# Attention's steps ahead of gl, weight sums in three chunks, first loads of sums moved, in an attention and FFN kernel

## The chip, the cores and the metric

The kernel runs on one core of a Trainium2 chip. The metric is the time of one execution on the device, in microseconds. TensorE multiplies matrices, VectorE and ScalarE work elementwise, GpSimd does a few reductions and exchanges, and SyncE (SP) issues the DMA transfers. Each engine works through a list of its own; a wait at the head of a list holds what stands behind it.

## The reference

Inputs are q, k and v of shape (8, 8, 576, 64): batch, heads, sequence, head dimension; and two weights, `w_in` (512, 2048) and `w_out` (2048, 512). All is float32.

```python
def _attn_ref(q, k, v):
    q_s = softmax of q over the head dimension
    k_s = softmax of k over the sequence
    kv = np.einsum('bhsd,bhse->bhde', k_s, v)
    return np.einsum('bhsd,bhde->bhse', q_s, kv)

x = attn_out.transpose(0, 2, 1, 3).reshape(8 * 576, 512)
h = np.maximum(x @ w_in, 0.0)
return h * h @ w_out
```

(The two softmax lines stand for the subtraction of the maximum, the exponential and the division by the sum plus 1e-9.) The attention is linear: it needs one 64x64 block `kv` for each head, and then one product with q. The two products of the FFN are nearly all of the arithmetic.

## The kernel before

**The numbers.** A float32 product is done as three matmuls of pieces: each operand is split into a rounded high part and the rest (`xh` and `xl`, `gh` and `gl`, and the weights alike), and high by high, high by low and low by high are added up.

**The tiles.** The 4608 rows of x are cut into nine tiles of 512: eight of the first 512 positions of a batch, and one of the eight tails of 64. Tiles t = 0 to 4 (`WT = 5`) run the FFN plainly. For each of 16 slabs f of 128 columns of the hidden layer: `first` multiplies x by a slab of w_in (12 matmuls into a bank `h`; there are two such banks); `split_g` makes `r` (the relu, ScalarE), its square (ScalarE), the high part `gh` (a cast on ScalarE), and `gl = r - gh` (VectorE); `second` multiplies by a slab of w_out and adds into four banks `acc`. `second` runs two slabs behind (`LA = 2`), so a `gl` has two slabs of time until it is read. `gh` has two buffers.

**The joint blocks.** Tiles 5, 6 and 7, 8 form two joint blocks of 1024 rows. They use a scheme of seven products for a 2x2 product of blocks (Strassen and Winograd), with sums of blocks of x and of weights as operands. `first_products(k)` runs pairs n = 0 to 7 of slabs, seven products each; `second_products(k)` the product by w_out. The sums of weights are made once, in tiles 1 to 3, for three keys a tile (`KEYS`), and stored in DRAM as `w_sums` and `wo_sums`: `full_sums` (two additions of 128x512), `add_sums` (four of 128x256), `split_sums` (two casts on ScalarE), `rest_sums` (two subtractions), `keep_sums` (the stores). The joint blocks load them: `load_weights` (parts `a11`, `a12`, `s1` and so on, of w_sums) and `load_s` (of wo_sums). `g_b` holds what the first products leave for the second.

**The attention.** Batches 0 and 1 are done before and during tile 0, where a planner sets the order. Batches 2 to 7 are done in 12 chunks of two pairs of heads, beside the FFN of tiles 1 to 4. A chunk n has five steps i, one for each f (the table `turns`; f = 0 has none but in tile 1). `pairs_step` does the pieces: i = 0 ends the first pair of heads (`end_k`: k shifted by its maximum, then `ek`, the exponential) and loads k of the second (`qn`) and of the next chunk; i = 1 sums and exponentials of q, the maximum of k of the second pair (`km` on VectorE, then `kmx` on GpSimd), and the exchange `bst` between partitions by DMA; i = 2 ends the second pair; i = 3 loads q and v of the next chunk (and kt and v_tail, the tails, at the first pair of a batch); i = 4 takes the maximum of the next k. `pairs_first` does, at i = 3, the norm of q (`blocks_norm`) and its transposes (`blocks_turn`). On TensorE `kv_of` (at i = 3) multiplies `ek` with v, and `x_two` (at i = 4, banks `h_x` and `x`) multiplies q with `kv`; both stand within `second` of that f, behind c = 2. The finished x is stored to `x_raw` and loaded again when its tile begins. `qn` shares its place in the memory with that x, so its load waits for the store.

**The order.** Outside the planner, each engine's list is in the order of the calls. In the loop over f it is: `first`, pieces of the sums (`sums_step`), `pairs_first`, `second`, `split_g` with `gl`, then `pairs_step`, `sums_after`, and in tile 4 `ahead`, which prepares the first joint block (splits of x at f = 7, 9, 10, 12 and so on, and loads of weights). For f < 2 `split_g` stands ahead of `pairs_first`.

In the rows, L100 is the line of a helper that records most operations; L1302 is the matmul of `first_products`; names without their numbers are tiles.

Of the kernel before, what the change touches and what calls it, by code (L numbers as in the profile page):

```python
# [336 lines left out]
def attention_ffn(  # L337
# [1131 lines left out]
    def pairs_step(n, i):  # L1469
# [3 lines left out]
        if i == 0:  # L1473
            load_kq(*two, "k")
            end_k(*one)
            if later:
                load_kq(*later[0], "k")
            blocks_exp(*one)
        elif i == 1:
            blocks_sum(*one)  # L1480
            blocks_exp(*two)
            begin_k(*two)
            blocks_sum(*two)
            blocks_swap()
        elif i == 2:
            end_k(*two)
        elif later:
            if i == 3:
                for p in later:
                    load_q(*p)  # L1490
                if later[0][1] == 0:
                    load_tail(later[0][0])
                    load_tail_v(later[0][0])
                for p in later:
                    load_v(*p)
            else:
                begin_k(*later[0])
# [39 lines left out]
    def sums_step(t, f):  # L1537
# [5 lines left out]
        for key, at in SUMS_AT.get(t, ()):  # L1543
            if f == at[0]:
                full_sums(key)
            if f == at[1]:
                for n in range(3):
                    add_sums(key, n)
            if f == at[2]:
                add_sums(key, 3)  # L1550
            if f == at[3]:
                rest_sums(key)
            if f == at[4]:
                keep_sums(key)

    def sums_after(t, f):

        for key, at in SUMS_AT.get(t, ()):
            if f == at[2]:
                split_sums(key)  # L1560

    THRICE = (2, 3, 4, 5, 6), (7, 8, 9, 10, 11), (12, 13, 14, 15, 15)
# [21 lines left out]
    def ahead(f, x):  # L1584

        k = range(2)
        if f == 4:
# [5 lines left out]
            w_of[0] = weights(0)  # L1593
            load_weights(0, w_of[0], "a11", "s1", "a12", "s2")
# [12 lines left out]
        elif f == 12:  # L1607
            take("t3", V, made["b11"], made["t2"], made["b11"])
# [26 lines left out]
    for t in range(WT):  # L1635
        x_next, acc = x_tile(t + 1) if t < TB else None, begin_acc(t)
        parts = {}
        for f in range(NF):
            todo = turns[t, f] if t else None
            h = first(t, f, x)  # L1640
            sums_step(t, f)
# [24 lines left out]
            elif todo:  # L1666
                pairs_step(*todo)
# [275 lines left out]

    def begin_ring():
# [5 lines left out]
    def first_products(k):  # L1950

        old = None
        for n in range(PAIRS):
# [60 lines left out]
            if 0 < n < 5:  # L2014
                load_s("s1", 2 * n - 2)
                if n < 4:
                    load_s("s1", 2 * n - 1)
            elif n == PAIRS - 1:
# [154 lines left out]
```

## Time and profile before

| | |
|---|---|
| time, median of 3 runs | 846.75 us (845.94 to 846.88) |
| the profiled execution | 847.65 us |
| its span in the profile | 845.8 us |
| TensorE busy | 828.0 us, 98% of the span |
| its weight loads | 663.4 us, 78% |
| VectorE busy | 604.9 us, 72% |
| ScalarE busy | 494.9 us, 59% |
| GpSimd busy | 139.0 us, 16% |
| granted clock of TensorE, mean | 0.997 |

The profile was taken on one execution, and all times below are of its span, counted from its start. A busy time is the sum of the times in which an engine executed; matmuls are pipelined, so the 390 ns of one matmul overlap the next, and one starts every 0.227 us. "Idle before" is the time for which an engine stood still just before an instruction, with the one that released it behind the arrow. The granted clock is a share of 2.4 GHz. A window gives busy times of PE, PEld, DVE, ACT and POOL with their numbers of instructions, then the granted clock, the share of the DMA engines that was busy, and what they moved.

### The profile page before, as it was taken

The page shows a single profiled execution, that of the slowest core. Times are in us where ns is not written, and L with a number is a line of the kernel's source. Part 1 is how long each engine was busy: PE and PEld are TensorE (multiplying, and loading weights), DVE is VectorE, ACT ScalarE, POOL GpSimd, SP SyncE. Part 2 cuts the span into 40 slices and gives each one's busy share as a digit, 9 for nine tenths or more (in the row PEclk, how much of TensorE's full clock was granted, in tenths as well). Part 3 has the DMA queues.
Part 4 walks back from the last instruction along what each step waited for, and adds up shares of the span by engine and source line. Part 5 has one row for each costly group of instructions (what it writes and reads, how often), then busy time and mean ns, then how long its engine had stood idle before and what let it go on. Part 6 is the DMA issues. An engine that isn't in the chain of part 4 may idle for free.

```text
span 845.8 us, 12951 instructions
## 1 busy us (share of the span) xinstructions
PE 828.0 (98%) x4411; PEld 663.4 (78%) x4411; DVE 604.9 (72%) x1100; ACT 494.9 (59%) x890; POOL 139.0 (16%) x151
## 2 busy tenths in 40 slices
PE   8999999999999999999999899999999999999997
PEld 6677778788887787788887777888888887778886
DVE  6989966776676575685764666477798986675985
ACT  5988745555556447555555366476754546675442
POOL 5889980001001000000000000000310000000000
PEclk9999999999999999999999999999999999999999
DMA  9992024436527547356536542889866789989455
GB/s 289 385 358 82 26 43 117 105 82 167 153 103 166 134 131 218 88 170 162 157 108 163 174 127 71 276 278 294 324 258 189 210 243 268 286 297 371 127 178 97
DMA packets 230146, 158.08 MB, mean 187 GB/s; under 512 B 147392, under 2 KB 200128, under 8 KB 230080
## 3 DMA queue, kind: packets, MB, share of 16 engines
q1 hardware_dynamic: 224160, 155.55, 60.6%
q10 hardware_dynamic: 5920, 1.71, 0.9%
q8 instruction: 35, 0.57, 0.3%
q14 instruction: 31, 0.25, 0.1%
HBM read 106.95 MB, written 49.81 MB: 185 GB/s over the span
## 4 chain that ended last, share of the span: by engine, by line
PE 79%; DMA 8%; DVE 5%; SPq 3%; ACT 2%; issue 1%; DVEq 0%; ACTq 0%
PE acc L100 21%; PE out L1844 18%; PE h L100 17%; PE h L1302 14%; PE h_x L100 5%; SPq L100 3%; DMA w<-w_sums 3%; PE x L100 2%; PE kv L100 2%; DMA raw<-in_moe_w_in_dram 2%; DMA k<-in_k_dram 2%; DVE bst L100 1%; DVE q L100 1%; DMA own_a<-w_sums 1%; DMA w<-x_raw 0%
## 5 line engine op out<-in xcount | busy, mean ns | idle before, releaser
L100 PE MATMUL acc<-w,gh 128*128 128x512 f32 x632 | 198.7, 396 | 0.0
L100 PE MATMUL h<-xh,w 128*128 128x512 f32 x544 | 179.6, 393 | 0.8 <-ACT xh L100 0.8
L1844 PE MATMUL out<-w,w 128*128 128x512 f32 x636 | 148.9, 389 | 0.0
L100 PEld LDWEIGHTS acc<-w,gh 128*128 128x128 f32 x632 | 116.4, 188 | 29.6 <-issue 6.3
L1844 PEld LDWEIGHTS out<-w,w 128*128 128x128 f32 x636 | 119.3, 188 | 25.1 <-DVE w L100 0.3
L100 PE MATMUL acc<-w,gl 128*128 128x512 f32 x316 | 123.3, 390 | 0.0
L100 DVE TENSOR_TENSOR gl<-r,gh 128x512 fp32r<-128x512 f32 x64 | 44.2, 690 | 108.2 <-ACT gh L100 108.2
L100 PEld LDWEIGHTS h<-xh,w 128*128 128x128 f32 x544 | 102.1, 188 | 23.5 <-ACT xh L100 1.3
L100 PE MATMUL h<-xl,w 128*128 128x512 f32 x272 | 106.3, 391 | 0.1
L100 POOL PARTITION_ALL_REDUCE kmx<-km x24 | 22.7, 946 | 360.3 <-DVE km L100 360.3
L1302 PE MATMUL h<-w,w 128*128 128x512 f32 x288 | 70.2, 392 | 2.0 <-DMA w<-w_sums 2.0
L100 PEld LDWEIGHTS acc<-w,gl 128*128 128x128 f32 x316 | 59.4, 188 | 12.5
L1302 PEld LDWEIGHTS h<-w,w 128*128 128x128 f32 x288 | 53.5, 188 | 15.4 <-DMA w<-w_sums 3.2
L100 PEld LDWEIGHTS h<-xl,w 128*128 128x128 f32 x272 | 51.1, 188 | 11.9 <-DVE xl L100 1.5
L100 ACT ACTIVATE c<-c 128x512 f32<-128x512 f32 x76 | 48.1, 633 | 20.2 <-DVE c L100 17.7
L100 ACT ACTIVATE kv<-kv,ks 64x64 f32<-64x64 f32 x64 | 19.8, 310 | 57.5 <-DVE ks L100 55.6
L100 ACT CAST gh<-r 128x512 fp32r<-128x512 f32 x64 | 39.8, 621 | 16.3 <-PE acc L100 14.8
L100 ACT ACTIVATE q<-q 128x576 f32<-128x576 f32 (+1 forms) x32 | 21.5, 672 | 46.2 <-DVE q L100 36.4
L100 ACT CAST w<-w 128x1024 fp32r<-128x1024 f32 (+1 forms) x38 | 37.9, 1004 | 15.6 <-PE out L1844 8.6
L1302 PE MATMUL h<-w,ring 128*128 128x512 f32 x192 | 46.4, 390 | 0.4 <-DMA ring<-w_sums 0.4
L100 ACT ACTIVATE r<-h 128x512 f32<-128x512 f32 x68 | 40.1, 590 | 9.4 <-PE h L100 8.9
L100 DVE TENSOR_TENSOR c<-h,u 128x512 f32<-128x512 f32 x48 | 33.0, 687 | 17.6 <-ACT u L100 14.9
(229 smaller groups left out, 1383.0 us busy)
## 6 DMA issues: line engine op xcount, KB each, us to landing
w<-wo_sums SPq DMA_DIRECT2D x64, 256.0 KB, 3.5
g_b<-c SPq DMA_DIRECT2D x60, 256.0 KB, 4.8
w<-g_b SPq DMA_DIRECT2D x18, 512.0 KB, 7.2
raw<-in_moe_w_in_dram SPq DMA_DIRECT2D x16, 512.0 KB, 7.7
raw<-in_moe_w_out_dram SPq DMA_DIRECT2D x16, 512.0 KB, 8.4
w<-w_sums SPq DMA_DIRECT2D x32, 256.0 KB, 5.8
w_sums<-w SPq DMA_DIRECT2D x30, 256.0 KB, 3.1
v<-in_v_dram SPq DMA_DIRECT2D x56, 128.0 KB, 2.9
```

What stands on the lines that cost most here:

```text
L100: getattr(self.eng, op)(*map(real, args), **{k: real(a) for k, a in kwargs.items()})
L1302: nc.tensor.matmul(out=out.real(), lhsT=a[:, k * P:(k + 1) * P].real(), rhs=m[k].real(), start=(begin and k == 0 and i == 0), stop=(k == 1 ...
L1844: nc.tensor.matmul(out=banks[name][m].real(), lhsT=a[:, m * P:(m + 1) * P].real(), rhs=b[:, i, :].real(), start=fresh and j == i == k == 0 ...
```

## The change

1. The step of a chunk, but for i = 3, moves from the end of the loop over f to right behind `first`, ahead of the sums and of `split_g`. So its instructions on VectorE and ScalarE stand ahead of `gh` and `gl` of the same f (in slabs f >= 2, ahead of the whole of `split_g`). The step i = 3 stays where it was.
2. At i = 3 the loads of kt and v_tail stand ahead of those of q.
3. The sums of a key are made in three places, not five. For the first key of a tile the additions and casts are in f = 0 behind `gl`, the subtractions and the store in f = 2; for the second `full_sums` is in f = 4, the additions and casts in f = 5, the rest in f = 7; for the third in f = 9, 10 and 12. The casts and the stores stand at the end of their f.
4. In tile 4 the first loads of weights for joint block 0 move from f = 4 to f = 12.
5. `FIRST_S` says behind which pair n the parts of the first sums s1 of wo_sums are loaded: in the first joint block as before, behind pairs 1 to 4; in the second behind pairs 1, 5, 6 and 7.

```diff
@@ -1486,11 +1486,11 @@
             end_k(*two)
         elif later:
             if i == 3:
-                for p in later:
-                    load_q(*p)
                 if later[0][1] == 0:
                     load_tail(later[0][0])
                     load_tail_v(later[0][0])
+                for p in later:
+                    load_q(*p)
                 for p in later:
                     load_v(*p)
             else:
@@ -1541,25 +1541,27 @@
         if t >= 1 and j < NF // 2 and i == 3:
             begin_sums(j)
         for key, at in SUMS_AT.get(t, ()):
-            if f == at[0]:
+            for work, when in zip((full_sums, all_sums, rest_sums), at):
+                if f == when and f:
+                    work(key)
+
+    def all_sums(key):
+
+        for n in range(4):
+            add_sums(key, n)
+
+    def sums_after(t, f):
+
+        for key, at in SUMS_AT.get(t, ()):
+            if f == at[0] == 0:
                 full_sums(key)
+                all_sums(key)
             if f == at[1]:
-                for n in range(3):
-                    add_sums(key, n)
+                split_sums(key)
             if f == at[2]:
-                add_sums(key, 3)
-            if f == at[3]:
-                rest_sums(key)
-            if f == at[4]:
                 keep_sums(key)
 
-    def sums_after(t, f):
-
-        for key, at in SUMS_AT.get(t, ()):
-            if f == at[2]:
-                split_sums(key)
-
-    THRICE = (2, 3, 4, 5, 6), (7, 8, 9, 10, 11), (12, 13, 14, 15, 15)
+    THRICE = (0, 0, 2), (4, 5, 7), (9, 10, 12)
     SUMS_AT = {t: list(zip(KEYS[3 * t - 3:3 * t], THRICE)) for t in range(1, WT)}
     assert len(KEYS) <= 3 * (WT - 1)
 
@@ -1590,8 +1592,6 @@
             made["b12"], made["b22"] = (
                 [slabs[X_RAW + j].bitcast(F32)[:, i, :] for i in k] for j in range(2)
             )
-            w_of[0] = weights(0)
-            load_weights(0, w_of[0], "a11", "s1", "a12", "s2")
         elif f == 5:
             for i in k:
                 Y.dma_start(out=slabs[X_RAW + i].bitcast(F32), in_=x_raw[WT + 1, i])
@@ -1605,6 +1605,8 @@
         elif f == 10:
             split_x_of("b21")
         elif f == 12:
+            w_of[0] = weights(0)
+            load_weights(0, w_of[0], "a11", "s1", "a12", "s2")
             take("t3", V, made["b11"], made["t2"], made["b11"])
             split_x_of("t2")
         elif f == 14:
@@ -1638,6 +1640,8 @@
         for f in range(NF):
             todo = turns[t, f] if t else None
             h = first(t, f, x)
+            if todo and todo[1] != 3:
+                pairs_step(*todo)
             sums_step(t, f)
             if f < LA:
                 parts[f] = split_g(t, f, *h)
@@ -1663,7 +1667,7 @@
                 plan.due = f + SOON
                 step_after(1, f, x_next)
                 plan.due = None
-            elif todo:
+            elif todo and todo[1] == 3:
                 pairs_step(*todo)
             sums_after(t, f)
             if t >= TB and f == (5 if t == TB else 3):
@@ -1940,6 +1944,10 @@
         now["k"] += 1
         split_x_of(name)
         now["k"] -= 1
+
+    FIRST_S = (
+        {1: (0, 1), 2: (2, 3), 3: (4, 5), 4: (6,)}, {1: (0, 1), 5: (2, 3), 6: (4, 5), 7: (6,)},
+    )
 
     def begin_ring():
 
@@ -2011,11 +2019,9 @@
             load_weights(n + 2, w_of.get(n + 2), "s3")
             if n == PAIRS - 3:
                 load_raw("b11", 0, *(temp("v", f"raw_b11_{k}_{i}", att, 2) for i in range(2)))
-            if 0 < n < 5:
-                load_s("s1", 2 * n - 2)
-                if n < 4:
-                    load_s("s1", 2 * n - 1)
-            elif n == PAIRS - 1:
+            for j in FIRST_S[k].get(n, ()):
+                load_s("s1", j)
+            if n == PAIRS - 1:
                 for j in range(2):
                     load_raw("b22", j, raw_place("t3", j))
             old = z
```

TensorE's and GpSimd's lists are the same in both kernels, but for line numbers. Three places follow.

VectorE in tile 4, from `gl` of f = 6 (before) and of f = 5 (now) on, in chunk 10. `km` is the maximum of the second pair's k, `kmx` that over all partitions, `w` and `t_0` are the split and a difference for the joint block. Before:

```order
L100 TENSOR_TENSOR gl_6_4970<-r_6_4953,gh_6_4968 128x512
L100 TENSOR_REDUCE bst_0_4934<-q_0_4805 128x18
L100 TENSOR_REDUCE bst_0_4934<-q_1_4810 128x18
L100 TENSOR_TENSOR q_1_4810<-q_1_4810,bst_0_4934 128x576
L100 TENSOR_REDUCE km_1_4976<-qn_1_4925 128x128
L100 TENSOR_TENSOR km_1_4976<-km_1_4976,kt_4815 64x128
L100 TENSOR_REDUCE bst_0_4934<-q_1_4810 128x18
L100 TENSOR_TENSOR gl_7_5016<-r_7_4999,gh_7_5014 128x512
L100 TENSOR_TENSOR qn_1_4925<-qn_1_4925,kmx_1_4979 128x512
L100 TENSOR_TENSOR kt_4815<-kt_4815,kmx_1_4979 64x128
L100 TENSOR_TENSOR w_852<-x_4828,w_779 128x512 x2
L100 TENSOR_TENSOR t_0_5027<-w_668,x_4828 128x512 x2
```

The same place now:

```order
L100 TENSOR_TENSOR gl_5_4932<-r_5_4902,gh_5_4930 128x512
L100 TENSOR_REDUCE bst_0_4914<-q_0_4810 128x18
L100 TENSOR_REDUCE bst_0_4914<-q_1_4815 128x18
L100 TENSOR_TENSOR q_1_4815<-q_1_4815,bst_0_4914 128x576
L100 TENSOR_REDUCE km_1_4956<-qn_1_4905 128x128
L100 TENSOR_TENSOR km_1_4956<-km_1_4956,kt_4805 64x128
L100 TENSOR_REDUCE bst_0_4914<-q_1_4815 128x18
L100 TENSOR_TENSOR gl_6_4980<-r_6_4949,gh_6_4978 128x512
L100 TENSOR_TENSOR qn_1_4905<-qn_1_4905,kmx_1_4959 128x512
L100 TENSOR_TENSOR kt_4805<-kt_4805,kmx_1_4959 64x128
L100 TENSOR_TENSOR gl_7_5017<-r_7_4995,gh_7_5015 128x512
L100 TENSOR_TENSOR w_852<-x_4828,w_779 128x512 x2
```

`gl` of f = 6 stood ahead of the work on q and on the maximum of k, and stands behind it now; the split of `w` has `gl` of f = 7 right ahead of it, which stood ahead of the shift of `qn`.

ScalarE at the start of tile 1, f = 0 to 2. `sums_h_i` is the cast of the sums, `r` the relu and the square, `ek` the exponential of k. Before:

```order
L100 ACTIVATE r_0_1734<-h_0_1721 128x512
L100 ACTIVATE r_0_1734<-r_0_1734 128x512
L100 CAST gh_0_1737<-r_0_1734 128x512
L100 ACTIVATE ek_0_1745<-k_0_1607 128x2x4x64
L100 ACTIVATE kt_1643<-kt_1643 64x128
L100 ACTIVATE q_0_1527<-q_0_1527 128x576
L100 ACTIVATE r_1_1767<-h_1_1754 128x512
L100 ACTIVATE r_1_1767<-r_1_1767 128x512
L100 CAST gh_1_1770<-r_1_1767 128x512
L100 ACTIVATE q_1_1707<-q_1_1707 128x576
L100 ACTIVATE r_2_1801<-h_2_1788 128x512
```

The same place now:

```order
L100 ACTIVATE r_0_1734<-h_0_1721 128x512
L100 ACTIVATE r_0_1734<-r_0_1734 128x512
L100 ACTIVATE ek_0_1741<-k_0_1607 128x2x4x64
L100 ACTIVATE kt_1643<-kt_1643 64x128
L100 ACTIVATE q_0_1527<-q_0_1527 128x576
L100 CAST gh_0_1750<-r_0_1734 128x512
L100 CAST sums_h_i_1762<-sums_i_1757 128x512 x2
L100 ACTIVATE r_1_1778<-h_1_1765 128x512
L100 ACTIVATE r_1_1778<-r_1_1778 128x512
L100 ACTIVATE q_1_1707<-q_1_1707 128x576
```

`ek`, `kt` and `q` moved ahead of `gh` of f = 0, and the casts of the first key's sums, which stood in f = 4, stand ahead of the relu of f = 1.

SP in the second joint block, from pair 4's loads on. `w<-w_sums`, `own_a` and `ring` are loads for the first products, `w<-wo_sums` are the first sums of the second products, `g_b<-c` stores, `out_dram<-o` stores of the output. Before:

```order
L100 DMA own_a_7100<-w_sums_154 128x1024
L100 DMA w_543<-w_sums_154 128x512 x2
L100 DMA g_b_1_121<-c_2_7112 128x512
L100 DMA w_929<-wo_sums_144 128x2x256
L100 DMA w_1058<-wo_sums_145 128x2x256
L100 DMA out_dram<-o_2_7134 32x16x32 x4
L100 DMA g_b_1_125<-c_3_7149 128x512
L100 DMA g_b_1_129<-c_2_7159 128x512
L100 DMA w_1461<-w_sums_154 128x512
L100 DMA g_b_1_117<-c_2_7171 128x512
```

The same place now:

```order
L100 DMA own_a_7100<-w_sums_154 128x1024
L100 DMA w_543<-w_sums_154 128x512 x2
L100 DMA g_b_1_121<-c_2_7112 128x512
L100 DMA out_dram<-o_2_7132 32x16x32 x4
L100 DMA g_b_1_125<-c_3_7147 128x512
L100 DMA g_b_1_129<-c_2_7157 128x512
L100 DMA w_1461<-w_sums_154 128x512
L100 DMA g_b_1_117<-c_2_7169 128x512
```

The two loads `w_929` and `w_1058` of wo_sums are gone from here; they come behind pair 5 now, those of `w_1203` and `w_1314` behind pair 6.

## Rows read from the trace of the kernel before

Times are microseconds from the start of the span.

**Rows 1.** The page, busy time of each engine over the span.

```profile
PE 828.0 (98%) x4411; PEld 663.4 (78%) x4411; DVE 604.9 (72%) x1100; ACT 494.9 (59%) x890; POOL 139.0 (16%) x151
```

**Rows 2.** Waits of TensorE: engine, line, what for; us in total, times, longest.

```profile
PE kv L100 <- ACT ek L100: 2.7, 2, 1.7
PE h_x L100 <- ACT kv L100: 2.0, 1, 2.0
PE h L1302 <- DMA w<-w_sums: 2.0, 3, 1.0
```

**Rows 3.** The page, groups: busy and mean, then idle time before and releaser.

```profile
L100 DVE TENSOR_TENSOR gl<-r,gh 128x512 fp32r<-128x512 f32 x64 | 44.2, 690 | 108.2 <-ACT gh L100 108.2
```

**Rows 4.** Timeline, tile 1, chunk 0: start, length, instruction, count, idle before.

```profile
138.60 0.69 DVE L100 TENSOR_TENSOR gl<-r,gh 128x512 fp32r<-128x512 f32 x1 [3.95 <-ACT gh L100]
...
142.17 0.58 ACT L100 ACTIVATE r<-h 128x512 f32<-128x512 f32 x1
...
144.62 0.39 PE L100 MATMUL h<-xh,w 128*128 128x512 f32 x1
...
148.81 1.27 DVE L100 TENSOR_TENSOR full_i<-w 128x512 f32<-128x512 f32 x2
...
152.00 0.69 PE L100 MATMUL kv<-v,ek 128*64 128x65 f32 x16 [1.74 <-ACT ek L100]
```

**Rows 5.** Timeline, the start of tile 4, ScalarE and TensorE.

```profile
427.70 2.17 ACT L100 CAST xh<-x 128x512 fp32r<-128x512 f32 x4
...
428.65 0.39 PE L100 MATMUL h<-xh,w 128*128 128x512 f32 x1
429.09 0.50 PE L100 MATMUL h<-xl,w 128*128 128x512 f32 x1
```

**Rows 6.** Timeline of VectorE, tile 2, chunk 4.

```profile
278.09 1.29 DVE L100 TENSOR_TENSOR full_o<-w 128x512 f32<-128x512 f32 x2 [3.33 <-DMA wo_sums<-sums_h_o]
```

**Rows 7.** Timeline, tile 4, chunk 10: SP, TensorE, then VectorE.

```profile
460.38 0.38 SPq L100 DMA_DIRECT2D x_raw<-x  x1
...
468.36 0.38 SPq L100 DMA_DIRECT2D qn<-in_k_dram  x1
...
473.40 0.39 PE L100 MATMUL acc<-w,gl 128*128 128x512 f32 x1
...
472.04 1.09 DVE L100 TENSOR_REDUCE km<-qn 128x128 f32<-128x512 f32 x1 [3.71 <-DMA qn<-in_k_dram]
...
474.04 0.67 DVE L100 TENSOR_TENSOR gl<-r,gh 128x512 fp32r<-128x512 f32 x1
...
476.72 1.29 DVE L100 TENSOR_TENSOR w<-x,w 128x512 fp32r<-128x512 f32 x2 [1.20 <-ACT w L100]
...
479.13 0.46 DVE L100 TENSOR_TENSOR bst<-bst 128x36 f32<-128x36 f32 x2
```

**Rows 8.** Windows: length, busy by engine, granted clock, DMA share, GB/s.

```profile
140.00:160.00 20.00, 18.24 (x131) 14.51 (x129) 14.79 (x33) 9.85 (x21) 0.70 (x1) 1.00 0.30 82
...
485.00:489.30 4.30, 4.28 (x27) 2.86 (x27) 0.72 (x3) 4.14 (x10) 0.00 (x0) 0.62 0.77 128
...
760.00:782.00 22.00, 22.00 (x99) 18.22 (x98) 12.48 (x15) 12.97 (x19) 0.00 (x0) 1.00 1.00 375
```

**Rows 9.** Timeline, tile 3, chunk 7, VectorE and TensorE.

```profile
371.93 1.07 DVE L100 TENSOR_REDUCE km<-qn 128x128 f32<-128x512 f32 x1
...
376.83 0.39 PE L100 MATMUL acc<-w,gl 128*128 128x512 f32 x1
```

**Rows 10.** Timeline of TensorE, second joint block, pairs 5 and 6.

```profile
729.63 2.20 PE L1302 MATMUL h<-w,w 128*128 128x512 f32 x9
732.27 0.96 PE L1302 MATMUL h<-w,ring 128*128 128x512 f32 x3 [0.44 <-DMA ring<-w_sums]
...
740.86 1.52 PE L1302 MATMUL h<-w,ring_s 128*128 128x512 f32 x6
742.73 1.65 PE L1302 MATMUL h<-w,w 128*128 128x512 f32 x6 [0.35 <-DMA w<-w_sums]
```

More of the change, by code (lines that the diff above doesn't have):

```diff
@@ L1543, in sums_step @@
         for key, at in SUMS_AT.get(t, ()):
-            if f == at[0]:
-                full_sums(key)
-            if f == at[1]:
-                for n in range(3):
-                    add_sums(key, n)
-            if f == at[2]:
-                add_sums(key, 3)
-            if f == at[3]:
-                rest_sums(key)
-            if f == at[4]:
-                keep_sums(key)
+            for work, when in zip((full_sums, all_sums, rest_sums), at):
[4 more added lines that the diff above has]
+            add_sums(key, n)
     def sums_after(t, f):
         for key, at in SUMS_AT.get(t, ()):
+            if f == at[0] == 0:
+                full_sums(key)
+                all_sums(key)
+            if f == at[1]:
+                split_sums(key)
             if f == at[2]:
-                split_sums(key)
-    THRICE = (2, 3, 4, 5, 6), (7, 8, 9, 10, 11), (12, 13, 14, 15, 15)
+                keep_sums(key)
+    THRICE = (0, 0, 2), (4, 5, 7), (9, 10, 12)
     SUMS_AT = {t: list(zip(KEYS[3 * t - 3:3 * t], THRICE)) for t in range(1, WT)}
```

## The prediction

> **What bounds the kernel now.** I read the page's table of busy time first: TensorE is busy for 828.0 us of a span of 845.8 us [rows 1], so at most 17.8 us can come from waits, and no other engine is near that. A change that leaves TensorE's list of instructions as it is can only win back waits, or open new ones. The second view is the list of waits of TensorE [rows 2]: it waits twice on the softmax of k (2.7 us), once on the scaled kv blocks (2.0 us), and three times on weight sums that are loaded in the joint blocks (2.0 us). The rest is the start and the end of the program and pieces of a few tenths. The third view says why the attention is late there: before `gl`, VectorE stands idle for 108.2 us in all, each time for the cast `gh` of ScalarE [rows 3]. VectorE works through its list in order, so the attention's steps that stand behind `gl` in the list wait with it, although a `gl` is read by TensorE only long after: one that ends at 466.2 is read from 473.40 on (part E). So the slack is on `gl`, and the step of the chunk is what is short of time. The change swaps the two in the list. What each swap is worth is read from the timelines of the places where TensorE waits.
>
> **Part A: chunk 0, in tile 1.** TensorE waits 1.74 us for `ek` at 152.00 [rows 4]. The chain ahead of it: the first piece of the sums (`full_i`, 1.27 us) and `gl` (0.68 us) stand on VectorE between the maximum of k and its shift; both leave the front of it, which is 1.95 us against a wait of 1.74 (both durations in [rows 4]), so the wait goes. The price is new: the first key's sums now stand whole in f = 0, and their casts ahead of the relu of f = 1 on ScalarE (the order in the section on the change). That relu frees the bank into which TensorE puts `h` of f = 3 at 144.62 [rows 4]. The relu's end, worked out: `gl` of f = 0 ends at 139.29 now; `ek`, `kt` and `q` come ahead of its cast on ScalarE, some 1.5 us (an estimate: three steps, two of them as long as the relu, one half of it), so it ends at 140.7; then on VectorE `full_i` (1.27) and four sums of half its tile's width (about 0.4 each, the same kind of step on half the elements of 0.64), to 143.6; then on ScalarE two casts of 0.54 each (four take 2.17 [rows 5]) and the relu's 0.58 [rows 4], to 145.3. It is 0.65 us late; 0.4 to 1.1 us by how the pieces overlap. Net 1.74 - 0.65 = 1.1 us (0.6 to 1.4). In tiles 2 and 3 f = 0 holds no step of the attention, so the 1.5 us are not there, the relu ends 0.8 us ahead of the read, and I count nothing.
>
> **Part B: starts of tiles 2 and 4.** The casts of the next x stand on ScalarE behind an attention step of f = 15. They begin at 427.70, right behind it, and TensorE's second matmul of tile 4 starts 0.44 us after the first [rows 5], where matmuls follow one another every 0.227 us (12 of an f in 2.72 us): 0.21 us lost, and about 0.1 on the next, at each of two starts. The attention's step now comes ahead of the last `gl`, so the casts start earlier: 0.6 us for both (0.4 to 0.65).
>
> **Part C: chunk 4, in tile 2.** `full_o` waits for the end of the last key's store and starts at 278.09 after 3.33 us of idle time [rows 6]; behind it stand `gl`, the shift of k and `ek`, and TensorE waits for that `ek`: 2.7 us on two waits, the longest 1.7, leave 1.0 for this one [rows 2, 6]. In the new order the maximum, the shift and `ek` of this chunk have no piece of the sums between them, and the next key's `full_o` waits behind them instead. Gain 1.0 us (0.9 to 1.6, with the pieces around it).
>
> **Part E: chunk 10, in tile 4.** Here is the largest single wait, 2.0 us ahead of `h_x` [rows 2], and behind it TensorE runs for 4.3 us at a mean granted clock of 0.62 [rows 8], which is its lower level, 1.2 GHz, for most of that time; at full clock the same work takes 0.62 x 4.3, so 1.6 us more are lost. The chain, from the rows: `x_raw` is stored from 460.38 on; the load `qn` shares its place with that x and is issued at 468.36, 8.0 us later; it lands at 472.04, after 3.71 us in which VectorE waits; then come the maximum, the shift, a split and a difference for the joint block (from 476.72), and the norm at 479.13 [rows 7]. With the step ahead of `gl`, the chunk before ends its norm some 2.2 us earlier (its `gl` with 0.69 us and the idle time of 2 us ahead of it leave its front), and with kt and v_tail ahead of q in SP's queue `x_raw` is issued at about 457.0. With the same 8.0 us, and the 3.7 us for the load, `qn` lands at 468.6. VectorE can then start the split as soon as ScalarE's casts end, and the norm at about 477.0, 2.1 us earlier: the wait is closed but for 0.1 to 0.4 us, and a gap so short is followed by no lower clock elsewhere in this trace (nor is the one of 1.74 us: the clock is 1.00 in 140 to 160 [rows 8]). Gain 2.0 + 1.6 less 0.1 to 0.4: I take 3.4 (0.5 to 4.5).
>
> What this adds: `gl` of f = 6 now stands behind `qn`'s maximum. Now the steps from the maximum to the end of a `gl` take from 472.04 to 474.71, 2.7 us; so it ends at 471.3, and TensorE reads it at 473.40 [rows 7]; there are 2.1 us to spare. In chunk 7 the same sum is smaller: its `qn` had landed by 371.93, and the read comes at 376.83 [rows 9].
>
> **Part F: the joint blocks.** Five loads of first sums (256 KB each) leave pairs 2, 3 and 4 of the second block for pairs 5, 6 and 7. SP then has two issues fewer, and 512 KB less are under way, ahead of the loads of `a11` for which TensorE waits in pairs 5 and 6. The rows of TensorE: 9 matmuls from 729.63 should end their issue at 731.67, and the next starts at 732.27, 0.6 us late; 6 from 740.86 give 742.22 against 742.73, 0.5 us [rows 10]. Both go: 1.1 us. Two more waits, in pairs 2 and 4 (the larger part of the 2.0 us [rows 2]), lie ahead of the moved loads or close behind them, and I leave them. Bounds: 0, if the loads are late for other reasons, and 3 with those two.
>
> On that, the Trainium skill, page "DMA: Bandwidth & Descriptors", section "Queues, rings and completion order", says that on each DMA engine descriptors are consumed in the order of the ring. By that rule what is issued ahead of a load delays it, which agrees with a gain here, and would make it some 1.4 us (512 KB at 375 GB/s, the rate of [rows 8]); by the rows of TensorE it stays 1.1 us.
>
> **Part G: what the moved loads meet.** From 760 to 782 the DMA engines are full (share 1.00, 375 GB/s), [rows 8], and what the second products read is loaded there. 1.28 MB more there is some 2 to 3 us of traffic at that rate, spread over 745 to 782. Each of their weights is cast before it is read, and at those casts TensorE does not wait in any row of the list of waits, which has no line for them [rows 2]; how much they may slip is between 0 and that traffic, so I put 0 us on it, bounds 0 to -1. The first loads of joint block 0 at f = 12 instead of f = 4 of tile 4 leave three f, some 16 us, until use, where `qn` took 3.7 us and `x_raw` to `qn` 8.0 [rows 7]: 0.
>
> **The sum.** A 1.1 + B 0.6 + C 1.0 + E 3.4 + F 1.1 + G 0 = 7.2 us. The profiled execution took 847.65 us and lies 0.9 us above the median of 846.75: 847.65 - 7.2 = 840.45 for a run like it, 839.5 on the median's scale.
>
> **The rivals.**
>
> Rival 1, slower: *`gl` waits for the attention*. What stands ahead of `gl` now carries its waits over. In chunks 4, 7 and 10 `qn` waits for a store. If `qn` lands 2.1 us late against 468.6, that is later than 470.7, `gl` misses its read, TensorE waits, and the clock may drop as it did behind the gap of 2.0 us: 3.6 us each time [rows 2, 8]. In chunk 10 alone (if `qn` still lands at 472.04, the read is 1.3 us late) that takes the whole of E and gives 843 to 844.5; in all three chunks it is 3 x 3.6 = 10.8 us against 7.2 - 3.4 = 3.8 us of gains left: 847.65 + 7.0 - 0.9 = 853.8. For two of them 850.2. For: 8.0 us from `x_raw` to `qn` is long, and I have moved only its start [rows 7]. Against: chunk 7 and chunk 4 have the landing before the point that decides, with the old timing already [rows 9].
>
> On this rival the Trainium skill, page "TensorE: Matmul & The Clock Gate", section "Architectural detail: the array is 16× 32×32, not 1× 128×128", says that the queues of ScalarE and VectorE are strictly first in, first out. By it nothing can overtake a waiting maximum; the idle time of 108.2 us before `gl`, with attention steps ready behind it, agrees.
>
> Rival 2: *chunk 10 stays bound*. The split and difference for the joint block stand ahead of the norm, and wait for ScalarE's casts (1.20 us at 476.72 [rows 7]). If these do not come earlier, E gives only the part of the lower clock or less, some 0.5 to 1: 842.0.
>
> Rival 3: *the joint block's waits are a backlog*, not the order of the loads; F is 0 and the waits move to the next pair: 840.6.
>
> Rival 4: *no more than the swap's own cost*: the bank of f = 3 is late in tiles 2 and 3 as well, and the new waits of A take 0.65 to 1.1 us in three tiles, with E gone as in rival 2: 844.5 to 846.5, which cannot be told from no change. What a measurement of this kernel can tell from no change is about 0.2%, 1.7 us.
>
> **How the numbers follow.** Forecast 839.5 with its own bounds (836 to 841.5, F and C at their ends) 0.54, and rival 3 lies inside them (0.10 of its own). Rival 2 and chunk 10 alone of rival 1, 842 to 844.5: 0.19. Rival 4: 0.08. Rival 1 in two chunks or more: 0.07. Less than 836, all at their upper ends: 0.02. The range holds 836.0 to 844.5, and about 0.83; it need not reach further. Faster by over 0.2% (under 845.05): 0.85. Within: 0.08. Slower: 0.07.
>
> **What would show it.** In the waits of TensorE, `kv` on `ek` and `h_x` on `kv` are gone, or below 0.5 us; a short wait of `h` on `r` at about 144.6 is new; the clock is 1.00 through 480 to 500. VectorE's idle time ahead of `gl` falls from 108.2 us by tens of us, and moves to no other line that TensorE waits on. `x_raw` of chunk 10 is issued near 457 and `qn` lands near 468.6. In the second joint block no wait in pairs 5 and 6. The forecast is wrong if TensorE waits for `gl` anywhere, if the lower clock is still in chunk 10, or if the splits of the second products now wait for loads longer than 3 us.

## The result

The changed kernel takes 839.25 us (median of 4 runs, 838.49 to 842.17), against 846.82 us of the kernel before (4 runs, 845.94 to 848.16) on the same chip: a ratio of 0.9916 with a 95% interval of 0.9888 to 0.9943, some 7.6 us less. Measured once more (e9), the ratio was 0.9903 (0.9869 to 0.9937). Forecast were 839.5 us, and 836.0 to 844.5. The time agrees; the working behind it agrees less, and the runs show where.

The profiled execution of the changed kernel took 838.49 us, its span is 836.7. Its table of busy time, which answers [rows 1], and its line for `gl`, which answers [rows 3]:

```profile
PE 824.2 (99%) x4411; PEld 661.7 (79%) x4411; DVE 604.0 (72%) x1100; ACT 493.6 (59%) x890; POOL 136.9 (16%) x151
...
L100 DVE TENSOR_TENSOR gl<-r,gh 128x512 fp32r<-128x512 f32 x64 | 44.2, 690 | 86.9 <-ACT gh L100 86.8
```

VectorE's idle time ahead of `gl` fell by 21 us and TensorE's busy time by 4 us. TensorE has the same 4411 instructions; some 2 of the 4 us are the matmuls of chunk 10 that ran at the lower clock (by the starts of the same instructions in both traces). Its list of waits, against [rows 2] (engine, line, what for; total, times, longest):

```profile
PE h L1302 <- ACT u L100: 1.4, 2, 0.7
...
PE h L1302 <- DMA ring<-w_sums: 0.6, 2, 0.3
PE h L1302 <- DMA w<-w_sums: 0.4, 1, 0.4
PE out L1848 <- DVE w L100: 0.4, 1, 0.4
PE h L100 <- ACT r L100: 0.2, 1, 0.2
```

The two waits on the attention, `kv` on `ek` and `h_x` on `kv`, are gone. The small one of `h` on `r` that was foretold for chunk 0 is there. The waits on `u` grew from 0.3 to 1.4 us: one of 0.71 us, in pair 7 of the second joint block, is new; the other, in pair 1, is in all 14 traces (0.2 to 2.1 us). New is also one of `out` on `w`. Of the waits of pairs 5 and 6 that the forecast wanted gone, the one in pair 6 is, and 0.30 us (on `ring`) stay in pair 5. (The wait of `h` on `xh` of 0.8 us, in both lists, is at the start of the program.)

Chunk 10 after, timeline of SP and VectorE, beside [rows 7]:

```profile
453.30 0.38 SPq L100 DMA_DIRECT2D x_raw<-x  x1
...
460.79 0.38 SPq L100 DMA_DIRECT2D qn<-in_k_dram  x1
...
463.42 1.08 DVE L100 TENSOR_REDUCE km<-qn 128x128 f32<-128x512 f32 x1 [5.41 <-DMA qn<-in_k_dram]
...
465.41 0.67 DVE L100 TENSOR_TENSOR gl<-r,gh 128x512 fp32r<-128x512 f32 x1
...
471.11 0.45 DVE L100 TENSOR_TENSOR bst<-bst 128x36 f32<-128x36 f32 x2
```

From the store of x to the issue of `qn` it is 7.5 us (8.0 before), and `qn` lands 2.6 us later (3.7 before). TensorE is 4.8 to 5.1 us earlier here than before, so `km`, 8.6 us earlier, has gained some 3.6 us on it. VectorE now waits 5.4 us for `qn` where it waited 3.7, and TensorE has no wait for VectorE here. The clock at this place, and in tile 1, beside [rows 8]:

```profile
140.00:160.00 20.00, 19.80 (x135) 15.07 (x134) 16.84 (x39) 11.09 (x24) 0.70 (x1) 1.00 0.51 144
...
471.00:478.00 7.00, 7.00 (x63) 5.69 (x63) 4.73 (x15) 2.02 (x6) 0.00 (x0) 1.00 0.20 33
```

**Where the time went, by place.** TensorE's list is the same in all kernels here, so the time between the starts of the same two of its instructions can be compared from trace to trace. The instructions are those that start at 140, 460, 500 and so on in the kernel before; the first differences are what the forecast gave each stage.

| stage, by the times of before | before, us | after, us | gain | forecast |
|---|---|---|---|---|
| 0 to 140, same code | 140.07 | 139.77 | 0.3 | 0 |
| 140 to 460, chunks 0 to 9 (A, B, C) | 319.95 | 315.42 | 4.5 | 2.7 |
| 460 to 500, chunk 10 (E) | 40.11 | 35.62 | 4.5 | 3.4 |
| 500 to 540, chunk 11 | 39.91 | 39.05 | 0.9 | 0 |
| 540 to 705 | 165.00 | 165.20 | -0.2 | 0 |
| 705 to 752, second joint block to pair 6 (F) | 46.99 | 46.17 | 0.8 | 1.1 |
| 752 to 800, pair 7 and second products (G) | 48.05 | 49.73 | -1.7 | 0 |
| sum | | | 9.1 | 7.2 |

The two profiled executions lie 9.2 us apart and the medians 7.6: the changed kernel's is the fastest of its four runs, and that of before lies above the median of its four.

The loss of the last stage is a chain of four rows. SP, ScalarE and TensorE of the changed kernel, in pair 7 and the second products:

```profile
746.43 0.98 SPq L100 DMA_DIRECT2D w<-wo_sums  x2
747.51 0.41 SPq L100 DMA_DIRECT2D w<-g_b  x1
...
753.44 1.05 ACT L100 CAST w<-w 128x1024 fp32r<-128x1024 f32 x1 [2.74 <-DMA w<-g_b]
754.39 0.58 ACT L100 COPY u<-h 128x512 f32<-128x512 f32 x1
...
755.02 0.50 PE L1302 MATMUL h<-t4h,ring_a 128*128 128x512 f32 x1 [0.71 <-ACT u L100]
...
769.89 1.05 ACT L100 CAST w<-w 128x1024 fp32r<-128x1024 f32 x1 [3.03 <-DMA w<-g_b]
...
772.25 3.01 PE L1848 MATMUL out<-w,w 128*128 128x512 f32 x12 [0.35 <-DVE w L100]
```

The moved loads `w<-wo_sums` stand ahead of the load `w<-g_b` of b21 in SP's queue. ScalarE's cast waits 2.74 us for it, the copy `u` stands behind the cast on ScalarE, and TensorE waits for the bank that `u` frees. In the kernel before the same cast and copy are back to back:

```profile
761.41 1.03 ACT L100 CAST w<-w 128x1024 fp32r<-128x1024 f32 x1
762.44 0.59 ACT L100 COPY u<-h 128x512 f32<-128x512 f32 x1
...
778.40 1.05 ACT L100 CAST w<-w 128x1024 fp32r<-128x1024 f32 x1 [1.77 <-DMA w<-g_b]
```

The later cast waited there too, 1.77 us (at 778.40), without a wait of TensorE behind it; now it waits 3.03 us (at 769.89), and TensorE's `out` waits 0.35 us.

### The profile page after: what moved, and what is told of

It is laid out like the page before. It is cut to its first block, busy times and chain, and to the rows that moved or that the text cites. A ratio compares the mean times of both kernels' runs of the same rounds, so it can differ in the third digit from the quotient of the medians.

```text
span 836.7 us, 12977 instructions
## 1 busy us (share of the span) xinstructions
PE 824.2 (99%) x4411; PEld 661.7 (79%) x4411; DVE 604.0 (72%) x1100; ACT 493.6 (59%) x890; POOL 136.9 (16%) x151
## 3 DMA queue, kind: packets, MB, share of 16 engines
HBM read 106.95 MB, written 49.81 MB: 187 GB/s over the span
## 4 chain that ended last, share of the span: by engine, by line
PE 80%; DMA 8%; DVE 5%; ACT 2%; SPq 2%; issue 1%; POOL 0%; ACTq 0%; DVEq 0%; POOLq 0%
PE acc L100 26%; PE h L100 20%; PE h L1302 13%; PE out L1848 11%; PE h_x L100 5%; PE kv L100 3%; SPq L100 2%; PE x L100 2%; DMA w<-g_b 2%; DVE w L100 2%; DMA w<-w_sums 2%; DMA ring<-w_sums 1%; DMA out_dram<-o 1%; DMA k<-in_k_dram 1%; ACT w L100 1%
## 5 line engine op out<-in xcount | busy, mean ns | idle before, releaser
L100 POOL PARTITION_ALL_REDUCE kmx<-km x24 | 20.5, 855 | 350.7 <-DVE km L100 350.7
L1302 PE MATMUL h<-w,ring 128*128 128x512 f32 x192 | 46.6, 391 | 0.6 <-DMA ring<-w_sums 0.6
L1302 PEld LDWEIGHTS h<-w,ring 128*128 128x128 f32 x192 | 35.8, 188 | 9.0 <-DMA ring<-w_sums 0.7
```

Of the source, the lines that this page charges most:

```text
L100: getattr(self.eng, op)(*map(real, args), **{k: real(a) for k, a in kwargs.items()})
L1302: nc.tensor.matmul(out=out.real(), lhsT=a[:, k * P:(k + 1) * P].real(), rhs=m[k].real(), start=(begin and k == 0 and i == 0), stop=(k == 1 ...
```

## The experiments

Each is compared with the kernel before on the same chip. The stages are those of the table above, taken in the same way from each trace: chunks 0 to 9, chunk 10, F and G.

| kernel | ratio (95% interval) | chunks 0 to 9 | chunk 10 | F | G |
|---|---|---|---|---|---|
| before | 1 | 319.95 | 40.11 | 46.99 | 48.05 |
| changed | 0.9916 (0.9888 to 0.9943) | 315.42 | 35.62 | 46.17 | 49.73 |
| changed, once more (e9) | 0.9903 (0.9869 to 0.9937) | 315.65 | 35.20 | 45.81 | 49.81 |
| first sums back (e1) | 0.9901 (0.9872 to 0.9929) | 315.01 | 35.47 | 46.64 | 48.05 |
| late first sums (e2) | 0.9868 (0.9848 to 0.9888) | 315.28 | 35.65 | 46.09 | 48.25 |
| late, once more (e10) | 0.9876 (0.9842 to 0.9909) | 314.89 | 36.80 | 43.79 | 48.30 |
| steps only (e3) | 1.0069 (1.0045 to 1.0094) | 327.09 | 39.07 | 47.67 | 48.35 |
| sums only (e4) | 1.0125 (1.01 to 1.015) | 331.37 | 39.33 | 46.88 | 48.05 |
| loads at f = 4 (e5) | 0.9921 (0.99 to 0.9943) | 315.25 | 36.68 | 46.85 | 50.52 |
| q first (e6) | 0.992 (0.9896 to 0.9944) | 315.81 | 35.97 | 46.52 | 50.05 |
| steps and sums (e7) | 0.9908 (0.9882 to 0.9934) | 315.47 | 36.55 | 46.99 | 48.05 |
| later first sums (e8) | 0.9867 (0.9842 to 0.9892) | 315.11 | 35.20 | 45.65 | 48.70 |
| later, once more (e11) | 0.9868 (0.9841 to 0.9894) | 315.37 | 35.65 | 46.32 | 48.49 |
| late sums on before (e12) | 0.9993 (0.9975 to 1.0012) | 319.33 | 37.79 | 47.95 | 48.05 |

**Is the late loss due to the moved loads?** The first kernel puts them back.

```diff
-    {1: (0, 1), 2: (2, 3), 3: (4, 5), 4: (6,)}, {1: (0, 1), 5: (2, 3), 6: (4, 5), 7: (6,)},
+    {1: (0, 1), 2: (2, 3), 3: (4, 5), 4: (6,)}, {1: (0, 1), 2: (2, 3), 3: (4, 5), 4: (6,)},
```

> The changed kernel with its first loads of sums in the second joint block put back behind pairs 2, 3 and 4. Theory (the moved loads help pairs 5 and 6 by some 0.6 to 1.1 us and cost 1.4 us later, because they stand ahead of the loads of b21 for which ScalarE's casts wait): the waits of TensorE in pair 7 (0.7 us) and in the second products (0.35 us) are gone, those of pairs 5 and 6 (some 0.4 us each) are back, and the time is 0.2 to 0.8 us shorter than that of the changed kernel. Rival (the two late waits have nothing to do with these loads but come from the program running 9 us earlier): both stay, and the time is 0.6 to 1.1 us longer.

The stage of G is 48.05 us again, to the last digit that of the kernel before, so its 1.7 us are the moved loads' and the rival falls. The waits of pairs 5 and 6 are back (0.46 and 0.32 us), and the stage of F is 46.64 us against 46.17, a difference that other pairs of traces don't bear out (below). The ratio, 0.9901, cannot be told from the changed kernel's 0.9916 and 0.9903.

The second kernel keeps loads 2 and 3 behind pair 5 and moves 4, 5 and 6 behind all loads of b21.

```diff
-    ..., {1: (0, 1), 5: (2, 3), 6: (4, 5), 7: (6,)},
+    ..., {1: (0, 1), 5: (2, 3)},
...
             elif s == 3:
-                load_s("s1", PAIRS - 1)
+                for n in range(4 if k else PAIRS - 1, PAIRS):
+                    load_s("s1", n)
```

> The changed kernel, with the first sums of weights 4, 5 and 6 of the second joint block loaded at step 3 of the second products, where that of weight 7 is loaded already, so behind all loads of b21. Theory: the relief of pairs 5 and 6 stays, the cast of b21 no longer waits 2.7 us, the waits in pair 7 and in the second products go: 1.0 to 1.4 us shorter than the changed kernel. Rival (late waits have another cause): no change. Second rival (the sums now come too late for the phase t1): a new wait of TensorE some 25 us on, at the 9th to 11th step of the second products, over 0.5 us.

It gave 837.23 us (837.10 to 837.37) against a median of 848.07 before. Timeline of SP and ScalarE at the place:

```profile
746.38 0.38 SPq L100 DMA_DIRECT2D w<-g_b  x1
...
767.06 4.07 SPq L100 DMA_DIRECT2D w<-wo_sums  x4
...
750.56 1.03 ACT L100 CAST w<-w 128x1024 fp32r<-128x1024 f32 x1
751.59 0.59 ACT L100 COPY u<-h 128x512 f32<-128x512 f32 x1
```

The first cast waits for nothing, and 73 matmuls of the second products run without a gap. G is 48.25 us, and no wait opens at the ninth to eleventh step. The gain in that stage is 1.5 us, a little over the theory's 1.0 to 1.4. One part of the theory did not hold: in pair 6 TensorE waits 0.78 us for `w<-w_sums`, where the changed kernel has no wait.

**Which edit carries the gain of tiles 1 to 4?** First the steps ahead of `gl` alone, on the kernel before.

```diff
             h = first(t, f, x)
+            if todo and todo[1] != 3:
+                pairs_step(*todo)
             sums_step(t, f)
...
-            elif todo:
+            elif todo and todo[1] == 3:
                 pairs_step(*todo)
```

> The kernel before with the first edit alone: the attention's steps ahead of gl, sums still in five places, loads as before. Theory (the steps ahead of gl make the chain of every chunk earlier; this edit gives chunk 10 and the tile starts, and the places of the sums give chunks 0 and 4): chunk 10 gains 3 to 4.5 us, the tile starts 0.6 us, chunk 0 and chunk 4 some part of 1.7 and 2.2 us: 4 to 7 us in all. Rival (without the sums out of the way, the steps find the same waits, and gl is late): under 3 us, with waits of TensorE for gl.

Neither came: it is slower, by 0.7%. Its waits of TensorE, and the place of the longest, in chunk 8 (SP, VectorE, TensorE):

```profile
PE h_x L100 <- ACT kv L100: 5.9, 3, 2.9
...
PE acc L100 <- ACT gh L100: 1.2, 1, 1.2
```

```profile
403.42 2.51 SPq L100 DMA_DIRECT2D bst<-bst  x4
405.98 2.20 SPq L100 DMA_DIRECT2D w_sums<-w  x4
408.23 0.61 SPq L100 DMA_DIRECT2D wo_sums<-sums_h_o  x1
...
412.27 1.29 DVE L100 TENSOR_TENSOR full_o<-w 128x512 f32<-128x512 f32 x2 [7.47 <-DMA wo_sums<-sums_h_o]
...
416.06 0.46 DVE L100 TENSOR_TENSOR bst<-bst 128x36 f32<-128x36 f32 x2
...
421.46 1.37 PE L100 MATMUL h_x<-qT,kv 64*64 64x64 f32 x7 [2.93 <-ACT kv L100]
```

The same place before:

```profile
397.67 2.15 SPq L100 DMA_DIRECT2D w_sums<-w  x4
399.86 1.12 SPq L100 DMA_DIRECT2D wo_sums<-sums_h_o  x1
...
403.99 2.49 SPq L100 DMA_DIRECT2D bst<-bst  x4
...
404.18 1.29 DVE L100 TENSOR_TENSOR full_o<-w 128x512 f32<-128x512 f32 x2 [0.22 <-DMA wo_sums<-sums_h_o]
```

The exchange `bst` of e3 stands ahead of the stores of a key's sums in SP's queue, where it stood behind them. The next key's `full_o` waits for that store's buffer, 7.47 us, and the chunk's norm stands behind `full_o` on VectorE. Chunk 0 and chunk 4 did gain (1.9 and 1.2 us at their `kv`), and chunks 5, 7 and 8 lost more, with the clock falling behind the gaps in chunks 7 and 8. In chunk 10 a wait of 1.37 us stays, with the lower clock behind it, and the chunk takes 39.07 us: this edit alone did not give the 3 to 4.5 us there that the theory had.

Then the sums in three places alone, the loop as in the changed kernel and the steps at the end of f.

```diff
-    THRICE = (2, 3, 4, 5, 6), (7, 8, 9, 10, 11), (12, 13, 14, 15, 15)
+    THRICE = (0, 0, 2), (4, 5, 7), (9, 10, 12)
```

> The kernel before with the third edit alone: sums in three places, the attention's steps still at the end of f. Theory: chunk 4 gains its 1 to 2 us, because full_o no longer stands ahead of gl and of the shift of k; chunk 0 gains 1.3 us less the bank of h of f = 3; chunk 10 keeps its wait of 2 us and its stretch at half clock, as no sums are made there: 2 to 3.5 us in all. Rival (chunk 10's wait comes from the work on sums in tile 3 or the stores of it): its wait falls below 1 us and the gain is over 5 us.

Slower by 1.25%. Waits, then VectorE and TensorE in tile 2, and the window behind the wait:

```profile
PE kv L100 <- ACT ek L100: 9.0, 3, 3.4
...
PE h L100 <- ACT r L100: 1.3, 1, 1.3
```

```profile
253.85 1.28 DVE L100 TENSOR_TENSOR sums_o<-sums_o,sums_h_o 128x512 fp32r<-128x512 f32 x2
255.05 0.69 DVE L100 TENSOR_TENSOR gl<-r,gh 128x512 fp32r<-128x512 f32 x1
255.65 0.69 DVE L100 TENSOR_TENSOR qn<-qn,kmx 128x512 f32<-128x512 f32 x1
...
257.05 0.69 PE L100 MATMUL kv<-v,ek 128*64 128x65 f32 x16 [2.88 <-ACT ek L100]
...
256.80:261.50 4.70, 4.45 (x29) 3.58 (x30) 2.99 (x9) 1.89 (x5) 0.00 (x0) 0.64 0.86 300
```

The sums of f = 0 and 2 stand ahead of `ek` in the first chunk of tiles 1, 2 and 3, and TensorE waits for it 2.7 to 3.4 us each time, with a mean clock of 0.62 and 0.64 behind the first two and of 1.00 behind the third. Here too the theory's sign was wrong; chunk 4's gain is there (1.5 us) and does not pay for it. In chunk 10, which this edit does not touch, the wait is 1.59 us and the lower clock stays.

So I formed a new one: the two need each other. The third kernel of the group has both, and neither the order of the tails, nor the later first loads, nor the moved sums.

> The first and the third edit together, without the other three. Each alone was slower than the kernel before. Theory (the two need each other: with the sums made early in f = 0, 4 and 9, no store waits behind the exchange of the next chunk and no full sum ahead of the norm; with the steps ahead of gl no sum stands ahead of ek): no wait of kv, none of h_x in chunks 5, 7 and 8, and the whole gain of the changed kernel up to tile 4, some 4.5 us, with chunk 10 as in the run with q first. Rival (one of the other edits is needed too): waits of kv or h_x over 1 us in tiles 1 to 3.

Chunks 0 to 9 take 315.47 us, as in the changed kernel, and there is no wait of `kv` or of `h_x`: each edit alone costs 7 and 11 us in that stage, and both together gain 4.5. The new theory holds. VectorE's rows agree: `full_i` and `full_o` wait 3.7 to 7.5 us for a store at six of nine keys in e3, 3.3 and 0.2 us at two keys before, and at none in e7 and in the changed kernel.

**The two small edits.** The first loads for joint block 0 back at f = 4 (item 4 of the change, reversed):

> The changed kernel without its fourth edit: the first loads for joint block 0 (1 MB) are issued at f = 4 of tile 4 again, right behind x_raw of chunk 10. In the changed kernel qn was issued 7.5 us after x_raw and landed at 463.4; gl of f = 6 stood behind it and ended 2.2 us ahead of its read. Theory (what is issued behind x_raw hardly delays it, and SP waits for the store anyway): qn is issued within 1 us of that, lands up to 1.5 us later, the slack of gl takes it, and TensorE's time in chunk 10 differs by under 0.5 us. Rival (the 1 MB holds the store or qn's load): qn lands over 2 us later, TensorE waits for gl or h_x in chunk 10, and it costs 2 to 4 us.

```profile
453.69 0.38 SPq L100 DMA_DIRECT2D x_raw<-x  x1
...
460.93 0.38 SPq L100 DMA_DIRECT2D qn<-in_k_dram  x1
...
464.60 1.07 DVE L100 TENSOR_REDUCE km<-qn 128x128 f32<-128x512 f32 x1 [6.46 <-DMA qn<-in_k_dram]
```

Between the two: the store is not delayed (7.2 us to the issue of `qn`), as the theory had it, but the load of `qn`, issued behind the 1 MB, takes 3.7 us instead of 2.6, and chunk 10 takes 1.1 us more, which is over the theory's 0.5 and under the rival's 2. In e7, which has this load back too, it takes 36.55 us. Of the seven traces whose code is the changed kernel's up to there, six have 35.20 to 35.65 us and one (e10) 36.80, so a cost of some 1 us is likely, but not certain. And with q ahead of the tails in SP's queue:

```diff
                 for p in later:
                     load_q(*p)
                 if later[0][1] == 0:
                     load_tail(later[0][0])
                     load_tail_v(later[0][0])
```

> The changed kernel without its second edit: q ahead of kt and v_tail in SP's queue again. In the changed kernel kt was issued at 441.5, as soon as the old kt was free, and q at 444.8, 3.3 us later. Theory (q's place is free only after the transposes, so the two loads of the tails, 3.2 us, used up time in which SP waited): x_raw of chunk 10 is issued 2 to 3 us later, qn lands near 466, gl of f = 6 and the norm are late, and TensorE loses 2 to 4 us in chunk 10 (a wait of h_x, clock below 1 behind it) and under 0.5 us elsewhere. Rival (the steps ahead of gl alone make the chain early enough): under 0.5 us in chunk 10.

Chunk 10 takes 0.35 us more, which is within those seven; the rival was right, and the theory's 2 to 4 us were far off.

**Still later first sums.** The next kernel moves two more pairs of loads:

```diff
-    ..., {1: (0, 1), 5: (2, 3)},
+    ..., {5: (0, 1)},
...
-                for n in range(4 if k else PAIRS - 1, PAIRS):
+                for n in range(2 if k else PAIRS - 1, PAIRS):
```

> As the run with the late first sums, and those of weights 2 and 3 go to step 3 of the second products as well, those of 0 and 1 from pair 1 to pair 5. Theory (each pair's wait comes from what SP issues ahead of its loads): the wait of 0.5 us in pair 4 falls below 0.2 us, pair 7 and the second products stay without a wait, and it is 0.3 to 0.8 us shorter than that run. Rival (the sums for the 9th step land too late): a new wait of over 0.5 us near 775 to 785.

836.62 us against 848.62 before. The wait that the theory named, in pair 4, is in neither late version's trace (it is 0.37 us in the changed kernel's). The one in pair 6 is 0.47 us, where it was 0.78; a wait of 0.35 us opened in the second products, against the theory and under the rival's 0.5, and G rose from 48.25 to 48.70. Then all three were measured on one chip:

> The changed kernel as it is, on the same chip as the next two, so that they can be compared. All theories: 7 to 9 us faster than the kernel before, with a wait in pair 7 (0.7 us) and one in the second products (0.35 us) of the second joint block.

> The kernel of the run with the late first sums once more. Theory: 1.0 to 2.0 us shorter than the changed kernel of the same call. Rival (what it showed in its own call was the chip or the start of the program): within 0.5 us of the changed kernel.

> The kernel of the run with the still later first sums once more. Theory: 0.3 to 0.8 us shorter than the one with the late first sums. Rival: the same within 0.3 us.

The medians are 839.60, 838.07 and 837.41 us, with ranges of 836.47 to 845.14, 834.22 to 842.39 and 836.61 to 838.34. The order agrees with the first measurements (839.25, 837.23, 836.62), and the stage of G shows where the late versions gain on the changed kernel: 1.5 and 1.3 us. Between the two late versions the runs do not decide.

**Is F worth anything without the rest?** The late sums on the kernel before:

> The kernel before with the late first sums and nothing else. Theory (the gain in the joint block is independent of the rest of the program): the waits of pairs 5 and 6 fall from some 1.1 us to under 0.5 us and no new one opens: 0.5 to 1.5 us shorter than the kernel before. Rival (the relief is there only when the rest of the program is earlier): no change.

No change: 848.67 against 848.52 us. The stage of F took 47.95 us, with 2.0 us of waits for `w` and 0.6 for `ring`, so the theory fell. With both main edits, kernels with moved loads have 43.79 to 46.85 us there (mean of eight 45.9), and the two with the loads in the old place 46.6 and 47.0; e3 and e4, with the loads in the old place and one main edit, have 47.67 and 46.88. The waits of pairs 5 and 6 together are 0 to 1.03 us with moved loads and both main edits (mean of eight 0.57), 0.68 to 1.23 with the loads in the old place (five traces), and 1.30 in e12. So a relief of F, of up to 1 us, may be there with the rest; how much of it belongs to the loads stays open.

## Why the prediction was right, by its steps

- **Its frame held.** The gain is time that TensorE spent on late operands, with the lower clock behind one of the gaps, and VectorE's `gl` had the slack that the steps needed. The largest single places were the right ones, and no wait for `gl` appeared (rival 1 did not happen): `gl` of f = 6 ended at 466.1, where its read came at 468.6.
- **A** (1.1 us forecast): the wait of 1.74 went, and the bank of f = 3 cost 0.2 us of idle time (some 0.45 by the starts of the matmuls), not 0.65. ScalarE had `ek`, `kt` and `q` behind it earlier than I counted, so the relu of f = 1 ended at 144.6, not 145.3. Net 1.5 us.
- **B** (0.6): the starts of tiles 2 and 4 gained 0.4 and 0.3 us.
- **C** (1.0): the wait gave 1.2 us, and another 0.9 us came as pieces of 0.15 to 0.34 us at the transposed blocks behind it. I had those only in the upper bound.
- **E** (3.4): 4.5 us in this pair of traces, 2.1 at `h_x`, 0.3 at `kv`, 2.0 behind it at the lower clock. I had taken the lower clock from one window, as 1.6 us. But the wait itself differs between executions of the same code: in e12, whose code is that of before up to there, it is 1.35 us and the clock stays at 1.00, and the stage takes 37.8 us, not 40.1. So against that execution E is worth 2.2 us. The store of x took 6.9 us there and 8.0 in the trace that I forecast from. The lower clock is also not in every execution of before: the mean clock of its 41 runs beside the experiments is 0.9976, against 0.9990 in 11 runs of the changed kernel, which over 848 us makes some 1.2 us (an estimate, in which the clock of all other places stands too). The chain within E was partly luck: set on the times of before, `x_raw` was issued near 458.2, not 457.0, and the load of `qn` took 2.6 us, not 3.7, because item 4 of the change, which I had priced at 0, took the 1 MB out of its way; both together put its landing near the 468.6 of the forecast. That kt stands ahead of q, on which I had counted, is not needed (e6).
- **F** (1.1): 0.8 us in this pair, with 0.30 us of wait left in pair 5. Rival 3, F at 0 with the waits moving on, is not ruled out: on the kernel before the late loads gave nothing (e12), and with both main edits waits of 0.3 to 1.03 us stay in pairs 5 and 6 of seven of eight traces.
- **G** (0, bounds 0 to -1) is the step that failed. It measured -1.7 us, and -2.5 and -2.0 in e5 and e6. I had weighed the casts of the second products, which have some room, and missed that the first of them stands in pair 7, ahead of the copy `u` on ScalarE, where a wait for the load is passed on at once. Part G of the forecast named 2 to 3 us of traffic (1.28 MB at 375 GB/s are 3.4) and then priced it at nothing since no row of before showed a wait: but the change itself adds to the queue there. A cast's wait of over 3 us for its load was one of the forecast's own signs of being wrong, and it came: 3.03 us at 769.89.
- **The sum** came out at 839.5 against 839.25 because A, C, E and chunk 11 (0.9 us, which I had not counted) were 4 us better, G 1.7 us worse, and the pair of executions 1.6 us further apart than the medians. That errors of this size cancel to 0.3 us is luck.
- **Added part by part**, as if the parts stood alone, the sum did no harm here, since every part was worked out in the full new order. But the parts do not add: e3 and e4 show that, taken over the stage, the gains of chunks 0 to 9 exist only for both edits together; in chunk 10 the steps alone left a wait of 1.37 us (e3), and both together none (e7). Rival 4's kind of cost, and worse, is what each edit has alone.
- Rival 2 did not happen: the norm of chunk 10 began at 471.11, and the split stood ahead of it without a wait.

## What to carry to other kernels

Before an instruction is moved ahead in one engine's list, ask what its DMA will then stand in front of in SP's queue, and who holds a buffer until that store has landed: two edits that are each slower alone can be faster together, so price them in the order that they make together. A load that is put off must not land in front of a more urgent one; put it behind the last load of the crowded stage, if its reader leaves the time. A cast that waits for a load passes its wait to all that stands behind it on its engine.

## What the runs showed of the hardware

- **The clock behind a gap.** Behind single gaps of TensorE of 2.0 us (before), 2.9 and 3.4 us (e4) stretches of 4 to 5 us have a mean granted clock of 0.62 to 0.64, so they ran for most of the time at the lower of the two levels, 1.2 and 2.4 GHz; so did the one behind a gap of 1.37 us (e3, 0.66). Behind gaps of 1.35 us (e12), 1.74 us (before) and 2.75 us (e4) it is 1.00. So the length of a gap alone does not tell whether the lower clock follows; what does, these runs do not show. The gaps of e12, e3 and e4 that go against their length, each with the window behind it:

```profile
482.00:486.30 4.30, 4.10 (x32) 2.65 (x33) 0.72 (x3) 4.12 (x10) 0.00 (x0) 1.00 0.82 133
...
492.52 0.66 PE L100 MATMUL h_x<-qT,kv 64*64 64x64 f32 x4 [1.37 <-ACT kv L100]
492.50:497.50 5.00, 4.96 (x30) 3.47 (x31) 1.96 (x5) 4.66 (x10) 0.70 (x1) 0.66 0.78 133
...
358.73 0.69 PE L100 MATMUL kv<-v,ek 128*64 128x65 f32 x16 [2.75 <-ACT ek L100]
358.50:363.00 4.50, 4.27 (x36) 3.59 (x37) 3.03 (x9) 1.70 (x5) 0.00 (x0) 1.00 0.84 297
```

- **A load waits for what is issued ahead of it, a store not for what is issued behind it.** With 1 MB of loads issued between the store of x and `qn`, the store took 7.2 us (e5; 7.5 without, in the changed kernel) and the load of `qn` 3.7 us (2.6 without). All 14 traces agree: the load took 3.45 to 3.71 us in the six with that 1 MB ahead of it and 2.60 to 2.85 us in the eight without; the store took 6.90 to 8.05 us in the six and 6.71 to 8.09 us in the eight. The Trainium skill, page "DMA: Bandwidth & Descriptors", section "Queues, rings and completion order", says that each DMA engine consumes descriptors in the order of its ring. The slower `qn` agrees with it, and so does the wait of 2.74 us in the stage of G.
- **Executions differ at the start.** The first 140 us, with the same code in all kernels, took 139.4 to 144.9 us in the 14 traces; in the three longest of them TensorE's wait for `sm`, ahead of `kmT`, was 2.2 to 3.7 us, in the others at most 1.4. In the two longest the granted clock fell there as well (0.66 in 56 to 61 of e1, 0.66 in 58.5 to 63.5 of e8). That is more than most parts of this change, and why stages were compared and not totals.
